# A list planner for attention plus FFN on one core: products picked by how they divide the array, a bias table built from low words, a flag computed inside the stream

## The chip, the cores and the metric

The kernel runs on one core of a Trainium2 chip. The metric is the device time of one launch in microseconds (us). The engines are PE (TensorE), DVE (VectorE), ACT (ScalarE), POOL (GpSimd) and SP (SyncE, which issues most DMAs). Every engine runs its own instructions in the order in which the program emitted them, and waits where an instruction's input or buffer is not ready.

## The reference

Attention with a causal window of 96 keys and 8 global keys, then a mixture of experts, then a second feed-forward network (FFN). B=2, H=8, S=768, head size 64; 4 experts 512 to 1024 to 512; last FFN 512 to 2048 to 512; everything in 32-bit floats.

```python
scores = scale * np.matmul(q, k.transpose(0, 1, 3, 2))
dist = np.where(is_global & ~is_local, float(n_local), np.abs(rel))
scores = scores - slopes[:, None, None] * dist
scores = np.where(is_global | is_local, scores, -1e9)
a = np.exp(scores - scores.max(-1, keepdims=True))
x = np.matmul(a / (a.sum(-1, keepdims=True) + 1e-09), v)      # to (1536, 512)
p = domain_probs / (domain_probs.sum(-1, keepdims=True) + 1e-09)
for e in range(4):
    out += p[:, e:e + 1] * (np.maximum(x @ w1[e], 0.0) @ w2[e])
h = out @ w_in
result = (h * np.clip(h + 3.0, 0.0, 6.0) / 6.0) @ w_out
```

## The kernel before

**Attention** is cut into 24 pairs of heads and query rows, in the order i = 0 to 23: batch b, then head pair hp, then chunk c of 256 rows (c 0 to 2 for the first batch, 3 to 5 for the second). A tile such as `at_4_3` is that of chunk 4, head pair 3. Each pair goes through these pieces: a load of q and k (`qkraw`, L323) and of v (L330) on SP; scores on PE (L351, operands of 64 rows in the two row halves of the array, `att_q<-qkraw 64*128`); bias, mask and minimum on DVE (L366); exponentials on ACT (L381); sums of the weights plus 1e-9, and reciprocals, on DVE (L392, L393); division on POOL (L401); transposes of the weights on PE (L420, the whole array, 128*128, called "turn"); copies of them out of PSUM (L437, ACT for one head's block and DVE for the other, L442 on ACT where the block is short); the product with v on PE (L457, 64 columns, the two column halves); a copy of its result to `xf` on ACT. A pair with c = 0 or 3 is "mixed": its first block sees 128 keys instead of 232, so its products are fewer.

**FFN.** A 32-bit product is made of three products of `fp32r` halves: high with high, low with high, high with low (L909, L913, L916 for the first layer, which runs 7 products for 8 by sums of operands, `wsum`, `xsum`; L1088, L1091, L1092 for the second). Weights and activations are split by a cast on ACT (L250: `w1h`, `w2h`, `xoh`, `hh`) and a subtraction on DVE (L255: `w1l`, `w2l`, `xol`, `hl`). The first layer of the first batch needs the 12 pairs of that batch; the remaining pairs run between its products. 4 experts and then the last FFN follow, in steps of a first and a second layer; from 97.04 us PE runs nothing but these products.

**The order** is made by `Plan`. Every piece of work has an engine, an assumed cost, predecessors and a rank. `emit` simulates the engines with these assumed costs (plus `LATENCY` between engines, `LOAD` behind a load), takes on each engine the ready piece of lowest rank, and emits it. Where the simulated PE would be idle by over 0.4 us, `keep_warm` emits dummy products (L263, `idle`) at that place in PE's stream. The result is one fixed order for each engine.

**The start and the end.** Sizes (n_global, n_local) come as 64-bit integers, two words each (`lo`, `hi`). DVE makes floats `nv` of both words, then the bias table `base` (L184 to L189, with `qkraw<-in_fast`, a table of distances). A flag says if the sizes fit the fast body; behind the body every engine loads it (L1199) and branches to a slow body if it is 0.

Of the kernel before, what the change touches and what calls it, by code (L numbers as in the profile page):

```python
# [21 lines left out]
P = 128  # L22
# [26 lines left out]
T_SCORES, T_TURN, T_VALUES = (0.95, 1.2), (0.8, 1.05), (0.75, 0.97)  # L49
# [9 lines left out]
class Plan:  # L59
# [8 lines left out]
    LATENCY = 0.25  # L68

    def __init__(self, idle=None):  # L70
        self.pieces = []
        self.ported = set()
        self.idle = idle

    def add(self, engine, cost, emit, after=(), rank=0.0, port=False):

        self.pieces.append((engine, cost, emit, after, rank))
        if port or engine == "pool":
            self.ported.add(len(self.pieces) - 1)
        return len(self.pieces) - 1  # L80
# [9 lines left out]
    def emit(self):  # L90
# [3 lines left out]
        port = 0.0  # L94
        for i, (engine, _, _, after, _) in enumerate(self.pieces):
# [50 lines left out]
def moe_attention_kernel(ctx, tc, qk, vw, sizes, dpt, w1, w2, w_in, w_out, ident_d, fast_d, slow_d, out):  # L146
# [29 lines left out]
    ng, nl, nl4 = nv[:, 0:1], nv[:, 1:2], nv[:, 6:7]  # L176
    flag = const.tile([P, 1], I32, name="flag")
    with tc.manual_schedule(engines={mybir.EngineType.DVE}):
        nc.vector.tensor_copy(nf[:], ni[:])
        nc.vector.scalar_tensor_tensor(out=nv[:, 2:4], in0=lo, scalar=0.0, in1=hi, op0=ALU.is_lt, op1=ALU.add)  # L180
        nc.vector.scalar_tensor_tensor(
            out=nv[:, 0:2], in0=nv[:, 2:4], scalar=4294967296.0, in1=lo, op0=ALU.mult, op1=ALU.add
        )
        nc.vector.tensor_scalar(out=window, in0=rel, scalar1=nl, scalar2=NONE, op0=ALU.is_ge, op1=ALU.mult)  # L184
        nc.vector.tensor_scalar(out=nl4, in0=nl, scalar1=-4.0, scalar2=None, op0=ALU.mult)
        nc.vector.scalar_tensor_tensor(out=window, in0=rel, scalar=-4.0, in1=window, op0=ALU.mult, op1=ALU.add)
        nc.vector.tensor_scalar(out=gidx, in0=gidx, scalar1=ng, scalar2=NONE, op0=ALU.is_ge, op1=ALU.mult)
        nc.vector.scalar_tensor_tensor(out=first, in0=gidx, scalar=nl4, in1=window[:, FAR:], op0=ALU.add, op1=ALU.max)
        nc.vector.scalar_tensor_tensor(  # L189
            out=global_keys, in0=gidx[:, :NG], scalar=nl4, in1=global_keys, op0=ALU.add, op1=ALU.max  # L190
        )
# [22 lines left out]
    def t_mm(n, count):  # L214
        return count * (0.0145 + n / 2400.0)

# [4 lines left out]
    def pools(bx, fast):  # L221
# [70 lines left out]
        def plan_bias(tabs, normalised):  # L292

            made = plan.add("dve", 1.9, lambda: None, (), -2.0)
            for h in range(H):
                for kind in range(2):
                    if h == 0:
                        started[h, kind] = made
                        continue

                    def scaled(h=h, kind=kind):
# [7 lines left out]
                        "pool", 0.46 if kind else 0.3, scaled, [made, normalised[3 * (h // 2) - 3] if h > 1 else None], (h // 2 * CPB - 2) * CH + 0.1 * h + 0.5 * kind  # L309
                    )  # L310

        def plan_pair(i, c, hp, tabs, place_users, normalised, biased, outs, x_bank):
# [43 lines left out]
            s_in = plan.add("pe", T_SCORES[kinds[0]], scores, [loaded] + waits, rank)  # L356
            readers.append(s_in)
            weighed = []
            for qb in range(CH):

                def bias(qb=qb, kind=kinds[qb], used=used[qb]):
# [3 lines left out]
                    for j in range(2):  # L365
                        nc.vector.tensor_tensor_reduce(  # L366
                            out=m["t"][:, qb, j, used], in0=m["s", j][:, qb * WIN : (qb + 1) * WIN][:, used],
                            in1=(base if hp == j == 0 else tabs[:, 2 * hp + j - 1])[:, kind * P : P + kind * WIN],
                            scale=-0.125, scalar=HUGE, op0=ALU.add, op1=ALU.min, accum_out=m["mn"][:, qb, j : j + 1],
                        )  # L370

                after = [s_in, started[2 * hp, kinds[qb]], started[2 * hp + 1, kinds[qb]]]
                e = plan.add("dve", 0.72 if kinds[qb] else 0.5, bias, after + wait_t, rank)
                for su in s_users:
                    su.append(e)
                biased[i].append(e)
# [9 lines left out]
                for j in range(2):  # L386
                    weighed.append(
                        plan.add("act", 0.48 if kinds[qb] else 0.39, lambda j=j, f=exponentials: f(j), [e], rank)
                    )

            def sums():
                nc.vector.tensor_scalar(out=m["sm"][:], in0=m["sm"][:], scalar1=1e-9, scalar2=None, op0=ALU.add)  # L392
                nc.vector.reciprocal(m["sm"][:], m["sm"][:])  # L393

            r = plan.add("dve", 0.4, sums, weighed, rank)
            normal = []
            for qb in range(CH):
                for j in range(2):
# [7 lines left out]
                    normal.append(plan.add("pool", 0.46 if kinds[qb] else 0.32, normalise, [r], rank))  # L406
# [7 lines left out]
            def turn(qb):  # L414
# [10 lines left out]
                plan.add("pe", 0.57 if kinds[qb] else 0.3, lambda qb=qb: turn(qb), normal[2*qb:2*qb+2] + wait_a[qb:qb+1], rank)  # L425
# [36 lines left out]
            v = plan.add("pe", T_VALUES[kinds[0]], values, [e for e, _ in copied] + [v_in, biased[i + 2] if b else outs[i - 2]], rank)  # L462
# [130 lines left out]
        def plan_ffn(attention):  # L593
# [513 lines left out]
            def plan_p(b, g):  # L1107
# [7 lines left out]
                gates[b, g] = (t, plan.add("load", 1.0, load, wait + [gate], 20.0 if b == g == 0 else -1.0), p_users)  # L1115

            def finish(b, last, ends):
# [3 lines left out]
                for d in range(KC):  # L1121
# [3 lines left out]
                    for n, part, after, cols, toks in lot:  # L1125
# [12 lines left out]
                        done.append(e)  # L1138
                        if last:
# [10 lines left out]

            results = {}
# [121 lines left out]
```

## Time and profile before

| what | value |
|---|---|
| time, median of 3 runs (lowest to highest) | 848.01 us (847.74 to 849.63) |
| time of the profiled execution | 847.26 us |
| its span in the trace | 845.2 us |
| PE busy | 833.7 us, 99% of the span |
| DVE, ACT, POOL busy | 78%, 48%, 8% |
| first attention product, first FFN product, first product of the second layer, last product | 4.99, 53.48, 97.04, 838.9 us |

The span is the part of the execution that the trace covers; 2.06 us of the profiled execution lie outside it. Busy shares are means over the whole span: attention, where all engines work together, is the first tenth of it only.

### The profile page before, as it was taken

How to read it: one execution, taken by the hardware profiler on the slowest of the kernel's cores; microseconds unless marked ns; L12 is line 12 of the kernel's file. 1: busy time of each engine (PE TensorE's matmuls, PEld its weight loads, DVE VectorE, ACT ScalarE, POOL GpSimd, SP SyncE). 2: the span in 40 equal slices, each digit the busy share in tenths (PEclk: the TensorE clock that was granted, in tenths of full speed). 3: DMA queues.
4: the chain of work that ended last, by engine and by line, in shares of the span. 5: the costliest groups of instructions: out<-in, count | busy, mean ns of one | idle time of the engine just before them, and what ended most of it. 6: DMA issues, size and time to landing. Idle time of an engine off the chain costs nothing.

```text
span 845.2 us, 13646 instructions
## 1 busy us (share of the span) xinstructions
PE 833.7 (99%) x5090; PEld 763.2 (90%) x5090; DVE 655.2 (78%) x1366; ACT 402.0 (48%) x850; POOL 68.1 (8%) x131
## 2 busy tenths in 40 slices
PE   8999999999999999999999999999999999999997
PEld 6777999999999999999999999999999999999996
DVE  6999989988998977987777688689898766545442
ACT  6998643543433433543333333335666455545441
POOL 5888200000000000000000000000000000000000
PEclk9999999999999999999999999999999999999999
DMA  7873454465565565645656664744452555534302
GB/s 264 314 221 94 175 202 153 138 211 181 166 209 194 165 222 180 204 150 179 216 172 199 208 208 158 234 165 140 174 163 103 172 186 185 190 125 139 136 1 79
DMA packets 56985, 147.34 MB, mean 174 GB/s; under 512 B 6480, under 2 KB 7760, under 8 KB 56912
## 3 DMA queue, kind: packets, MB, share of 16 engines
q1 hardware_dynamic: 56480, 145.69, 52.2%
q8 instruction: 42, 0.69, 0.3%
q10 hardware_dynamic: 432, 0.71, 0.3%
q14 instruction: 31, 0.25, 0.1%
HBM read 109.66 MB, written 36.72 MB: 173 GB/s over the span
## 4 chain that ended last, share of the span: by engine, by line
PE 92%; DMA 3%; DVE 2%; POOL 1%; ACT 1%; issue 0%; SPq 0%; POOLq 0%; DVEq 0%; ACTq 0%
PE o L1091 16%; PE o L1092 15%; PE o L1088 15%; PE x_x L909 8%; PE x_x L913 8%; PE x_x L916 8%; PE w_w L913 6%; PE w_w L916 6%; PE w_w L909 6%; PE att_q L420 2%; PE att_q L351 1%; PE att_q L457 1%; DMA qkraw<-in_qk 1%; DMA w<-qkraw 1%; POOL t L401 1%; PE att_x L457 1%
## 5 line engine op out<-in xcount | busy, mean ns | idle before, releaser
L1091 PE MATMUL o<-hh,w2l 128*128 128x512 f32 (+1 forms) x768 | 259.4, 338 | 0.0
L1092 PE MATMUL o<-hl,w2h 128*128 128x512 f32 (+1 forms) x768 | 259.0, 337 | 0.0
L1088 PE MATMUL o<-hh,w2h 128*128 128x512 f32 (+1 forms) x768 | 257.8, 336 | 0.0
L933 ACT COPY snap<-x_x 128x384 f32<-128x384 f32 x144 | 68.9, 478 | 195.9 <-PE x_x L916 195.7
L946 DVE TENSOR_TENSOR c_c<-w_w,snap 128x384 f32<-128x384 f32 x144 | 80.0, 556 | 104.4 <-ACT w2h L250 58.5
L1092 PEld LDWEIGHTS o<-hl,w2h 128*128 128x128 f32 x768 | 144.4, 188 | 16.0
L1088 PEld LDWEIGHTS o<-hh,w2h 128*128 128x128 f32 x768 | 144.4, 188 | 13.4
L1091 PEld LDWEIGHTS o<-hh,w2l 128*128 128x128 f32 x768 | 144.5, 188 | 12.7
L909 PE MATMUL x_x<-xoh,w1h 128*128 128x384 f32 x384 | 129.7, 338 | 0.1
L916 PE MATMUL x_x<-xoh,w1l 128*128 128x384 f32 x384 | 129.0, 336 | 0.0
L913 PE MATMUL x_x<-xol,w1h 128*128 128x384 f32 x384 | 128.9, 336 | 0.0
L913 PE MATMUL w_w<-xol,w1h 128*128 128x384 f32 x288 | 97.1, 337 | 0.0
L909 PE MATMUL w_w<-xoh,w1h 128*128 128x384 f32 x288 | 97.0, 337 | 0.0
L916 PE MATMUL w_w<-xoh,w1l 128*128 128x384 f32 x288 | 96.8, 336 | 0.0
L250 ACT CAST w2h<-wr 128x1024 fp32r<-128x1024 f32 x48 | 50.4, 1050 | 61.2 <-PE o L1092 59.1
L909 PEld LDWEIGHTS x_x<-xoh,w1h 128*128 128x128 f32 x384 | 72.3, 188 | 3.2 <-issue 0.6
L913 PEld LDWEIGHTS x_x<-xol,w1h 128*128 128x128 f32 x384 | 72.3, 188 | 2.0
L1015 ACT CAST hh<-c_c 128x384 fp32r<-128x384 f32 x96 | 49.4, 514 | 48.3 <-DVE c_c L984 47.8
L916 PEld LDWEIGHTS x_x<-xoh,w1l 128*128 128x128 f32 x384 | 72.0, 188 | 0.0
L250 ACT CAST w1h<-wr 128x512 fp32r<-128x512 f32 x96 | 46.9, 510 | 49.5 <-PE w_w L913 45.7
L255 DVE TENSOR_TENSOR w2l<-wr,w2h 128x1024 fp32r<-128x1024 f32 x48 | 58.5, 1219 | 2.3 <-ACT w2h L250 2.3
L984 DVE SCALAR_TENSOR_TENSOR c_c<-c_c,p 128x384 f32<-128x384 f32 x96 | 53.8, 561 | 3.2
(90 smaller groups left out, 1132.7 us busy)
## 6 DMA issues: line engine op xcount, KB each, us to landing
wr<-in_w SPq DMA_DIRECT2D x64, 512.0 KB, 3.9
wr<-w SPq DMA_DIRECT2D x32, 512.0 KB, 3.5
kept<-w1h SPq DMA_DIRECT2D x24, 512.0 KB, 3.0
kept<-w1l SPq DMA_DIRECT2D x24, 512.0 KB, 4.8
w1h<-kept SPq DMA_DIRECT2D x24, 512.0 KB, 3.7
w1l<-kept SPq DMA_DIRECT2D x24, 512.0 KB, 4.9
qkraw<-in_w_in SPq DMA_DIRECT2D x16, 512.0 KB, 4.3
w<-qkraw SPq DMA_DIRECT2D x32, 256.0 KB, 4.2
```

What stands on the lines that cost most here:

```text
L250: nc.scalar.copy(out_ap, src)
L255: nc.vector.tensor_tensor(out_ap, src, hi_ap.bitcast(F32), op=ALU.subtract)
L909: nc.tensor.matmul(ps_, wh[:, a, cols], xh[:, o, kc, :], start=start and kc == 0, stop=False, skip_group_check=True,)
L913: nc.tensor.matmul(ps_, wh[:, a, cols], xl[:, o, kc, :], start=False, stop=False, skip_group_check=True)
L916: nc.tensor.matmul(ps_, wl[:, a, cols], xh[:, o, kc, :], start=False, stop=last, skip_group_check=True)
L933: nc.scalar.copy(m["n", n][:], m["x"][:, :HT])
L946: nc.vector.tensor_tensor(m[name][:], m["w"][:, :HT], m["n", n][:], op=ALU.add)
L984: nc.vector.scalar_tensor_tensor(out=room_for(), in0=src(), scalar=0.0, in1=p["p"][:, cols], op0=ALU.max, op1=ALU.mult)
L1015: nc.scalar.copy(at(0), room_for())
L1088: nc.tensor.matmul(o, wh, hh, start=first and own and f == 0, stop=False, skip_group_check=True)
L1091: nc.tensor.matmul(o, wl, hh, start=False, stop=False, skip_group_check=True)
L1092: nc.tensor.matmul(o, wh, hl, start=False, stop=end, skip_group_check=True)
```

## The change

Six edits, all in what the planner is told or in when a piece is emitted; the arithmetic of the fast body stays the same.

1. **Modes.** Scores get mode "rows", values "columns", all other products none. PE now picks among its first 12 ready pieces the lowest of rank plus 3.0 where the mode differs from that of the last piece; a change of mode is charged 0.1.
2. **Assumed costs.** `LATENCY` 0.25 to 0.12; scores, values and transposes cheaper; bias pieces one head at a time.
3. **Low words.** The first pass uses the sizes' low words as they are; -4 times n_local is made on ACT; the table's global keys are a piece of their own behind the table; the assumed time of the table goes from 1.9 to 0.9.
4. **First pair.** Its sums are made block by block (two pieces).
5. **Flag.** The exact sizes and the flag are computed in the stream by DVE (`ask`, rank 100); the loads of the flag stand behind the first output copy instead of behind the body.
6. **Loads of the probabilities** (`p`) get ranks 34 and 100 for the first two of the first batch, before 20 and -1.

```diff
-T_SCORES, T_TURN, T_VALUES = (0.95, 1.2), (0.8, 1.05), (0.75, 0.97)
+T_SCORES, T_TURN, T_VALUES = (0.87, 1.15), (0.22, 0.45), (0.65, 0.86)
+SWITCH, SWITCH_RANK = 0.1, 3.0
-    LATENCY = 0.25
+    LATENCY = 0.12
+                if engine == "pe" and now[engine]:
+                    place = min(
+                        range(min(len(now[engine]), 12)),
+                        key=lambda k: now[engine][k][0] + SWITCH_RANK * (self.modes.get(now[engine][k][1]) != mode),
+                    )
+                    if best is None or free[engine] < best[0]:
+                        best = (free[engine], engine, place)
+                    continue
+            if engine == "pe" and self.modes.get(i) != mode:
+                mode = self.modes.get(i)
+                cost += SWITCH
...
+        nc.scalar.mul(nl4, nl_low, -4.0)
+        nc.vector.tensor_scalar(out=window, in0=rel, scalar1=nl_low, scalar2=NONE, op0=ALU.is_ge, op1=ALU.mult)
...
-            made = plan.add("dve", 1.9, lambda: None, (), -2.0)
+            made = plan.add("dve", 0.9, lambda: None, (), -2.0)
+            whole = plan.add("dve", 0.22, with_global, [made], 0.0)
...
-            s_in = plan.add("pe", T_SCORES[kinds[0]], scores, [loaded] + waits, rank)
+            s_in = plan.add("pe", T_SCORES[kinds[0]], scores, [loaded] + waits, rank, mode="rows")
-                e = plan.add("dve", 0.72 if kinds[qb] else 0.5, bias, after + wait_t, rank)
+                for j in range(2):
+                    after = [s_in, started[2 * hp + j, kinds[qb]]]
+                    e = plan.add(
+                        "dve", 0.32 if kinds[qb] else 0.21, lambda j=j, f=bias: f(j), after + wait_t, rank
+                    )
-            r = plan.add("dve", 0.4, sums, weighed, rank)
+            parts = [slice(qb, qb + 1) for qb in range(CH)] if i == 0 else [slice(0, CH)]
+            summed = [
+                plan.add("dve", 0.36, lambda part=part: sums(part), weighed[2 * part.start : 2 * part.stop], rank)
+                for part in parts
+            ]
-                plan.add("pe", 0.57 if kinds[qb] else 0.3, lambda qb=qb: turn(qb), normal[2*qb:2*qb+2] + wait_a[qb:qb+1], rank)
+                plan.add("pe", T_TURN[kinds[qb]], lambda qb=qb: turn(qb), normal[2*qb:2*qb+2] + wait_a[qb:qb+1], rank)
-            v = plan.add("pe", T_VALUES[kinds[0]], values, [e for e, _ in copied] + [v_in, biased[i + 2] if b else outs[i - 2]], rank)
+            v = plan.add("pe", T_VALUES[kinds[0]], values, [e for e, _ in copied] + [v_in, biased[i + 2] if b else outs[i - 2]], rank, mode="columns")
...
-                gates[b, g] = (t, plan.add("load", 1.0, load, wait + [gate], 20.0 if b == g == 0 else -1.0), p_users)
+                gates[b, g] = (t, plan.add("load", 1.0, load, wait + [gate], 34.0 if b == g == 0 else 100.0 if b == 0 and g == 1 else -1.0), p_users)
...
+                        if last and b == B - 1 and d == part == 0:
+                            plan.add(
+                                "act", 0.6, lambda: is_fast.append(nc.values_load(flag[0:1, 0:1], min_val=0, max_val=1)),
+                                [e], -9.0,
+                            )
...
+                plan.add("dve", 1.2, ask, x_ready[1], 100.0)
...
-    is_fast = nc.values_load(flag[0:1, 0:1], min_val=0, max_val=1)
-    with tc.If(is_fast == 0):
+    with tc.If(is_fast[0] == 0):
```

What this does to the orders is seen at three places.

PE, behind the first pair's scores. In the kernel before, `att_q2` and `att_q3` are the scores of pair 1, then `att_q0` and `att_q1` those of pair 2, and the transposes of pair 0 (`t_0_0`) come last:

```order
L351 MATMUL att_q2_250<-qkraw_62 128x232
L351 MATMUL att_q3_251<-qkraw_62 128x232
L263 LDWEIGHTS idle_85
L263 MATMUL w_ps_139<-idle_85 128x192
L263 LDWEIGHTS idle_85
L263 MATMUL w_ps_139<-idle_85 128x192
L351 MATMUL att_q0_210<-qkraw_62 128x232
L351 MATMUL att_q1_211<-qkraw_62 128x232
L351 MATMUL att_q0_210<-qkraw_62 128x232
L351 MATMUL att_q1_211<-qkraw_62 128x232
L420 MATMUL att_q4_282<-qkraw_62,t_0_0_221 128x128 x2
L420 MATMUL att_q5_292<-qkraw_62,t_0_0_221 128x128 x4
```

In the changed kernel the transposes of pair 0's first block stand ahead of pair 1's scores:

```order
L277 LDWEIGHTS idle_82
L277 MATMUL w_ps_136<-idle_82 128x192
L450 MATMUL att_q4_256<-qkraw_62,t_0_0_216 128x128 x2
L372 MATMUL att_q2_260<-qkraw_62 128x232
L372 MATMUL att_q3_261<-qkraw_62 128x232
L372 MATMUL att_q2_260<-qkraw_62 128x232
L372 MATMUL att_q3_261<-qkraw_62 128x232
L450 MATMUL att_q5_272<-qkraw_62,t_0_0_216 128x128 x4
L372 MATMUL att_q0_207<-qkraw_62 128x232
L372 MATMUL att_q1_208<-qkraw_62 128x232
L372 MATMUL att_q0_207<-qkraw_62 128x232
L372 MATMUL att_q1_208<-qkraw_62 128x232
```

So the scores of pairs 1 and 2 moved from ahead of the first transposes to behind them; the dummies between those scores are gone.

SP's queue in the middle of attention. The `qkraw` loads here are those of pairs 9, 10, 11 and 12; before:

```order
L323 DMA qkraw_62<-in_qk 128x624
L589 DMA p_dram_1_140<-gate_142 128x4x12
L1113 DMA p_0_1_459<-p_dram_1_140 128x768
L330 DMA v_0_2_473<-in_vw 128x512
L323 DMA qkraw_62<-in_qk 128x624
L1113 DMA p_0_0_502<-p_dram_1_140 128x768
L330 DMA v_1_2_515<-in_vw 128x512
L323 DMA qkraw_62<-in_qk 128x624
L775 DMA wr2_0_536<-in_w2 128x2x512
L330 DMA v_2_2_570<-in_vw 128x512
L775 DMA wr1_1_582<-in_w1 128x2x512
L323 DMA qkraw_62<-in_qk 128x624
```

And in the changed kernel, where the first row is the loads of pairs 8 and 9:

```order
L344 DMA qkraw_62<-in_qk 128x624 x2
L351 DMA v_2_1_424<-in_vw 128x512
L805 DMA wr1_0_430<-in_w1 128x2x512
L619 DMA p_dram_1_137<-gate_139 128x4x12
L344 DMA qkraw_62<-in_qk 128x624
L351 DMA v_0_2_484<-in_vw 128x512
L351 DMA v_1_2_500<-in_vw 128x512
L1143 DMA p_0_0_511<-p_dram_1_137 128x768
L344 DMA qkraw_62<-in_qk 128x624
L351 DMA v_2_2_545<-in_vw 128x512
L805 DMA wr2_0_556<-in_w2 128x2x512
L344 DMA qkraw_62<-in_qk 128x624
```

The load of `p_0_1` and that of the weights `wr1_1` no longer stand ahead of pair 12's load.

DVE near the end of attention, around the copies of the last transposes (`at_4_3_1` is that of pair 22, `at_5_3_1` that of pair 23); before:

```order
L984 SCALAR_TENSOR_TENSOR t_0_1_0_1407<-x_0_x_965,p_0_0_502 128x384
L255 TENSOR_TENSOR w1l_1_741<-wsum_1_1327,w1h_1_740 128x1024
L946 TENSOR_TENSOR c_0_c12_1437<-w_0_w_1164,snap_0_2_1225 128x384
L984 SCALAR_TENSOR_TENSOR c_0_c12_1437<-c_0_c12_1437,p_0_0_502 128x384
L255 TENSOR_TENSOR hl_0_1072<-c_0_c22_1386,hh_0_1071 128x384
L255 TENSOR_TENSOR hl_0_1072<-t_0_1_0_1407,hh_0_1071 128x384
L437 COPY at_4_3_1_1468<-att_q5_292 128x512
L946 TENSOR_TENSOR c_1_c11_1470<-w_1_w_1450,snap_1_1_1448 128x384
L255 TENSOR_TENSOR hl_0_1072<-c_0_c12_1437,hh_0_1071 128x384
L984 SCALAR_TENSOR_TENSOR c_1_c11_1470<-c_1_c11_1470,p_0_0_502 128x384
L255 TENSOR_TENSOR w1l_2_1435<-wr1_2_1382,w1h_2_1434 128x512
L437 COPY at_5_3_1_1500<-att_q5_292 128x512
```

And in the changed kernel:

```order
L1014 SCALAR_TENSOR_TENSOR t_0_1_0_1384<-x_0_x_998,p_0_0_511 128x384
L467 COPY at_4_3_1_1394<-att_q5_272 128x512
L417 TENSOR_SCALAR sm_5_3_1350<-sm_5_3_1350 128x4
L418 RECIPROCAL sm_5_3_1350<-sm_5_3_1350 128x4
L269 TENSOR_TENSOR hl_0_1142<-c_0_c22_1348,hh_0_1141 128x384
L976 TENSOR_TENSOR c_0_c12_1418<-w_0_w_1130,snap_0_2_1229 128x384
L1014 SCALAR_TENSOR_TENSOR c_0_c12_1418<-c_0_c12_1418,p_0_0_511 128x384
L269 TENSOR_TENSOR hl_0_1142<-t_0_1_0_1384,hh_0_1141 128x384
L269 TENSOR_TENSOR w1l_1_1325<-wr1_1_710,w1h_1_1324 128x512
L269 TENSOR_TENSOR hl_0_1142<-c_0_c12_1418,hh_0_1141 128x384
L269 TENSOR_TENSOR w1l_1_1325<-wr1_1_710,w1h_1_1324 128x256
L269 TENSOR_TENSOR w1l_1_1325<-wsum_1_1367,w1h_1_1324 128x1024
```

The three splits into `w1l_1`, weights of the second expert's step, all stand behind the copy of pair 22; before, the first two (512 and 256) stand some 140 instructions further up, the third just ahead of that copy.

## Rows read from the trace of the kernel before

**Rows 1.** The page: TensorE's granted clock in 40 slices, 9 is full.

```profile
PEclk9999999999999999999999999999999999999999
```

**Rows 2.** Busy time by stage: us, PE, PEld, DVE, ACT, POOL (x), PEclk, DMA share, GB/s.

```profile
4.99:25.38 20.39, 19.06 (x176) 13.69 (x176) 17.68 (x92) 16.15 (x64) 13.93 (x34) 1.00 0.78 261
25.38:53.48 28.10, 27.39 (x279) 20.68 (x278) 25.78 (x107) 27.25 (x96) 21.61 (x43) 1.00 0.98 341
53.48:97.04 43.56, 41.95 (x375) 34.53 (x374) 40.66 (x122) 36.00 (x112) 32.15 (x51) 1.00 0.42 125
97.04:838.90 741.86, 741.72 (x4243) 691.21 (x4242) 570.20 (x1043) 321.07 (x580) 0.00 (x0) 1.00 0.51 170
```

**Rows 3.** Timeline of PE, two stretches of attention: start, us, engine, line, xcount.

```profile
15.34 1.05 PE L351 MATMUL att_q<-qkraw 64*128 64x232 f32 x8
16.32 1.10 PE L457 MATMUL att_x<-at,v 104*64 104x128 f32 x16
17.35 1.09 PE L420 MATMUL att_q<-qkraw,t 128*128 128x128 f32 x8
18.37 0.89 PE L351 MATMUL att_q<-qkraw 64*128 64x128 f32 x8
...
92.14 0.66 PE L420 MATMUL att_q<-qkraw,t 128*128 128x128 f32 x4
92.55 0.42 PE L909 MATMUL w_w<-xoh,w1h 128*128 128x384 f32 x1
```

**Rows 4.** Timeline of the start, all engines, with idle time before and releaser.

```profile
1.05 3.56 PE L199 MATMUL w_ps<-idle 128*128 128x192 bf16 x22 [1.05 <-POOL idle L195]
...
5.84 1.58 PE L263 MATMUL w_ps<-idle 128*128 128x192 bf16 x17
...
7.28 0.40 ACT L381 ACTIVATE t<-t,mn 128x128 f32<-128x128 f32 x1 [4.60 <-DVE mn L366]
...
7.34 1.05 PE L351 MATMUL att_q<-qkraw 64*128 64x232 f32 x8
...
9.13 0.17 DVE L392 TENSOR_SCALAR sm<-sm 128x4 f32<-128x4 f32 x1 [0.99 <-ACT t L381]
...
9.69 1.59 POOL L401 TENSOR_SCALAR t<-t,sm 128x128 f32<-128x128 f32 x4 [2.16 <-DVE sm L393]
...
10.12 1.66 PE L420 MATMUL att_q<-qkraw,t 128*128 128x128 f32 x6 [0.46 <-POOL t L401]
```

**Rows 5.** Timeline of PE around 20 us, where the gate's pieces run on DVE.

```profile
20.83 0.66 PE L457 MATMUL att_x<-at,v 104*64 104x128 f32 x8 [0.52 <-DVE at L437]
```

**Rows 6.** Timeline of PE around the scores of pair 12.

```profile
36.15 0.60 PE L420 MATMUL att_q<-qkraw,t 128*128 128x128 f32 x4
37.45 0.89 PE L351 MATMUL att_q<-qkraw 64*128 64x128 f32 x8 [0.70 <-DMA qkraw<-in_qk]
...
42.23 0.88 PE L457 MATMUL att_x<-at,v 128*64 128x128 f32 x12
```

**Rows 7.** Casts of weights on ACT by line, then dummies in PE's timeline.

```profile
L250 ACT CAST w2h<-wr x2: 1034/1046/1058, 36.0 to 45.2; 128x1024 fp32r<-128x1024 f32 x2
...
49.89 0.58 PE L263 MATMUL w_ps<-idle 128*128 128x192 bf16 x5
```

**Rows 8.** Behind the first FFN product: PE's and DVE's timelines, and low halves on DVE by line.

```profile
62.30 0.63 PE L420 MATMUL att_q<-qkraw,t 128*128 128x128 f32 x4 [1.22 <-DVE at L437]
...
94.83 1.10 PE L457 MATMUL att_q<-at,v 104*64 104x128 f32 x16
...
92.83 0.69 DVE L437 COPY at<-att_q 128x512 f32<-128x512 f32 x1
...
L255 DVE TENSOR_TENSOR w2l<-wr,w2h x2: 1224/1232/1240, 37.0 to 46.4; 128x1024 fp32r<-128x1024 f32 x2
```

**Rows 9.** Loads of the flag behind the body: ns, and when.

```profile
L1199 PEldq TENSOR_LOAD <-flag x1: 758/758/758, 837.3 to 837.3; - x1
...
L1199 ACTq TENSOR_LOAD <-flag x1: 476/476/476, 840.7 to 840.7; - x1
```

More of the change, by code (lines that the diff above doesn't have):

```diff
@@ L72, in __init__, with add @@
         self.ported = set()
+        self.modes = {}
         self.idle = idle
-    def add(self, engine, cost, emit, after=(), rank=0.0, port=False):
+    def add(self, engine, cost, emit, after=(), rank=0.0, port=False, mode=None):
         self.pieces.append((engine, cost, emit, after, rank))
+        if mode:
+            self.modes[len(self.pieces) - 1] = mode
         if port or engine == "pool":
@@ L94, in emit @@
         port = 0.0
+        mode = None
         for i, (engine, _, _, after, _) in enumerate(self.pieces):
@@ L387, in plan_pair, with sums @@
                     weighed.append(
-                        plan.add("act", 0.48 if kinds[qb] else 0.39, lambda j=j, f=exponentials: f(j), [e], rank)
+                        plan.add("act", 0.48 if kinds[qb] else 0.39, lambda j=j, f=exponentials: f(j), [shifted[j]], rank)
                     )
-            def sums():
-                nc.vector.tensor_scalar(out=m["sm"][:], in0=m["sm"][:], scalar1=1e-9, scalar2=None, op0=ALU.add)
-                nc.vector.reciprocal(m["sm"][:], m["sm"][:])
-            r = plan.add("dve", 0.4, sums, weighed, rank)
+            def sums(part):
+                sm = m["sm"][:, part].rearrange("p a b -> p (a b)")
+                nc.vector.tensor_scalar(out=sm, in0=sm, scalar1=1e-9, scalar2=None, op0=ALU.add)
+                nc.vector.reciprocal(sm, sm)
+            parts = [slice(qb, qb + 1) for qb in range(CH)] if i == 0 else [slice(0, CH)]
[3 more added lines that the diff above has]
+            ]
             normal = []
@@ L1149, in finish, with ask @@
                 results[b] = done
+            if fast:
+                def ask():
+                    nc.vector.scalar_tensor_tensor(
+                        out=nv[:, 2:4], in0=lo, scalar=0.0, in1=hi, op0=ALU.is_lt, op1=ALU.add
+                    )
+                    nc.vector.scalar_tensor_tensor(
+                        out=nv[:, 0:2], in0=nv[:, 2:4], scalar=4294967296.0, in1=lo, op0=ALU.mult, op1=ALU.add
+                    )
+                    nc.vector.tensor_scalar(out=nv[:, 4:5], in0=nl, scalar1=1.0, scalar2=None, op0=ALU.is_ge)
+                    nc.vector.scalar_tensor_tensor(
+                        out=nv[:, 5:6], in0=nl, scalar=float(NPREV + 1), in1=nv[:, 4:5], op0=ALU.is_le, op1=ALU.mult
+                    )
+                    nc.vector.scalar_tensor_tensor(
+                        out=nv[:, 5:6], in0=ng, scalar=-2147483648.0, in1=nv[:, 5:6], op0=ALU.is_ge, op1=ALU.mult
+                    )
+                    nc.vector.scalar_tensor_tensor(
+                        out=flag[:], in0=ng, scalar=float(NG), in1=nv[:, 5:6], op0=ALU.is_le, op1=ALU.mult
+                    )
+                plan.add("dve", 1.2, ask, x_ready[1], 100.0)
             results = {}
```

51 lines of the change are left out of this document (20 added, 31 removed).

## The prediction

> **What bounds the kernel now.** I began with the stages [rows 2]. From 97.04 us to the last product PE is busy 741.72 of 741.86 us, so nothing that the change does there can shorten the time, unless it takes away products, and it takes away none. What can move are the 92 us before: three stretches in which PE is idle 1.33, 0.71 and 1.61 us, and in which some groups are stretched besides. PE is still the engine that paces them, but ACT is at 97% in the second stretch (27.25 of 28.10) and DVE at 93% in the third (40.66 of 43.56). Next I read PE's timeline for the price of a group, start to next start [rows 3]: scores 0.98 us, values 1.03, eight transposes 1.02, scores of a mixed pair about 0.82 and values of one 0.81 (estimates by their count of columns). Four transposes ahead of a whole-array product take 0.41; twice that is 0.82, so leaving the whole array after eight costs about 0.20. I then followed the start [rows 4], the copy that PE waits for at 20.8 [rows 5], the load at 37 [rows 6], the casts [rows 7], the waits behind the first FFN product [rows 8] and the end [rows 9].
>
> **The start: later, +1.0.** Before, the four exponentials of pair 0 run from 7.28 in the order 128, 128, 232, 232, and their sums start at 9.13; POOL divides from 9.69 (0.40 each), PE transposes from 10.12 [rows 4]. The new order is 128, 232, 128, 232 and sums per block, so the first block's sums wait for the third exponential: 7.28 + 0.40 + 0.48 + 0.40 = 8.6 with its read-out. 0.56 from sums to POOL gives 9.2, two divisions 10.0, the two transposes follow the divisions. The low words bring nothing here: the table waits for its distances, which land only at 5.40, and without the flag's interleaved instructions the first bias is at most 0.2 sooner. What moves is the other side: pair 1's scores stood ahead of those transposes at 7.34, now they stand behind them, at 10.2. PE idles from the end of the dummies (7.4) to about 9.7. In the prices of rows 3: 10.2 + scores 0.98 + four transposes 0.59 + scores 0.98 gives values of pair 0 at 12.8 (before 12.5), then mixed scores, two more score groups and two transpose groups, and values of pair 1 at 17.7 (before 16.32) [rows 3]. That is +1.4. Before, PE waits 0.52 at 20.83 for a copy that stands behind the gate's pieces on DVE [rows 5]; a later PE finds it done, which returns 0.5. I take +1.0. Bounds: 0 (the waits of this stretch, 1.33 idle plus stretched groups, absorb all) and +2.9 (10.2 less 7.34, nothing regained).
>
> **25 to 53 us: −1.5.** The load of pair 12's q and k has one load of probabilities (393 KB) and one of weights (512 KB) fewer ahead of it: 905 KB at this stretch's 341 GB/s [rows 2] is 2.65 us, more than the 0.70 that PE waits for it [rows 6]. From 36.15 to the values at 42.23 PE spends 6.08 us on two score groups, one values group and fourteen transposes, which cost 0.98 + 0.82 + 1.03 + 14 x 0.128 + 0.2 for their pieces = 4.8 by rows 3; 1.3 goes. The order also moves the two `w2h` casts (2.1 us of ACT) behind the first FFN product, with their low halves on DVE (2.5 us) [rows 7, 8]. ACT sets PE's waits where dummies stand in the stream, the five at 49.89 the largest (0.5); I give 0.9 for these. New waits: a copy behind a 1024-wide subtraction on DVE and values of pair 14 behind theirs, 0.35 each by the timeline, 0.7. Sum −1.5. Bounds −2.2 (no new waits) and 0.
>
> **53 to 97 us: −0.2.** The moved casts and subtractions fall here. Waits that go: 1.22 at 62.30 and the rest of the 1.61 idle [rows 2, 8], with the stretched groups some 2.4. Waits that come, from the order: transposes of pair 18 behind their sums (0.6), the copy behind `w2l` (1.23, of which 0.35 is not covered), the products of the second step behind `w1l_1`, which now stands behind the copy of pair 22 and four other pieces (0.95 of 0.5 + 1.3 not covered), the last copy (0.35). 2.25 against 2.4. Six first-layer products (78 before, 72 now) move behind the first second-layer product; at 0.175 (741.86/4243) that shifts 1.05 us from one side of that point to the other and changes no time. Bounds −2.1 (all old waits gone, no new) and +2.4 (all come on top).
>
> **Grouping: inside these terms.** I counted PE's changes of mode up to the second layer in the two orders: 82 and 78, of which leaving the whole array 35 and 33. Two times 0.20 is 0.4; where a group merges, its waits merge too, so −0.1 is in the sums above and 0.4 is the bound of this edit. The Trainium skill, TensorEngine Tiling (Array Packing), section "Key Properties", says that a change of tiling mode drains TensorE, without a figure. If each of the four changes cost the 0.20 of the row, the sum would be 0.7 lower; the trace shows the cost at leaving the whole array only, so that is a part of rival C.
>
> **The end: −0.5.** Before, ACT loads the flag at 840.7, behind its output DMA, 0.48 us [rows 9], and its branch is the last thing of the span. Now the load is behind the first output copy, beside products; PE's own sequencer reached it at 837.3, 1.6 us ahead of its last product, so a load inside the stream stops no product. Bounds −0.5 and 0. The six flag instructions in DVE's stream (0.15 each, 1 us) come behind x of the second batch, at about 97, where DVE is 77% busy.
>
> **Sum.** +1.0 − 1.5 − 0.2 − 0.5 = −1.2. The profiled execution took 847.26, so 846.1; the median of the runs stands 0.75 above it, and the median should go from 848.01 to 846.8.
>
> **Rivals.**
> *B, DVE becomes the bound after the first FFN product (slower).* That product comes 2.8 us later (56.2), and 2.5 us of low halves plus the rest come with it into a stretch that is 93% busy. If DVE reaches some 97%, its pieces are late one after the other: the last copy, at 92.83, comes at 96.1, and the last values, 94.83 [rows 8], at 96.2, +1.3; with the six products that are then behind instead of ahead, 1.05, and the end's −0.5, +1.9: 849.9. For it: the DVE share. Against it: PE waited for DVE once only.
> *C, the late start is caught up.* PE idles anyway in the first stretch, and groups merge. Then +1.0 is 0 to 0.3, and the later terms reach two thirds of their bounds: 843.4 to 845.5. For it: more pieces per block, so less idling behind sums; against it: PE shows 19.06 of 20.39 busy, little room.
> *D, the clock falls at the start.* The granted clock is full in all slices [rows 1], that is the upper of 1.2 and 2.4 GHz, and before the longest idle of PE is 1.22. Yet the first 22 dummies took 0.162 each, the 17 later 0.093 [rows 4]. The new order lets PE idle 2.3 us at 7.4. If products again run at the early pace for 3.56 us, 1.5 is lost: 848.3. The Trainium skill, TensorE: Matmul & The Clock Gate, section "Why this matters for your kernels", warns that idle gaps of PE lower the clock; no row before shows it.
> *E, no change that adds up*: the planner's new costs move waits and remove none, 848.0.
>
> **How the numbers follow.** Forecast 0.45 (its own range 845.3 to 848.3), C 0.22, B 0.17, D 0.08, E 0.08. A measurement of this kernel tells 0.2%, 1.7 us, from nothing: faster is under 846.3, slower over 849.7. Faster: all of C and two fifths of the forecast, 0.40. Slower: most of B and the forecast's upper edge, 0.17. The rest 0.43. The range 843.4 to 849.6 goes from C's low end to just short of B.
>
> **What would show it.** Start right: pair 1's scores near 10.2 with 2.3 of PE idle before, values of pair 1 near 17.7. Second stretch right: no DMA wait before pair 12's scores, first FFN product near 56. Third: first product of the second layer near 95.3 (97.04 − 1.05 − 0.7). End: the last product near 838, ACT's last instruction the output DMA. Wrong: scores of pair 1 still near 7 or PE clock under full at 8 to 12 (D); last values past 96 with DVE at 97% (B); the second layer before 94 (C).

## The result: 1.2% slower, most of it in one place at 700 us

The changed kernel took 859.09 us (median of 4 runs, 857.25 to 860.48) against 848.1 for the kernel before on the same chip: ratio 1.0123, 95% interval 1.011 to 1.0137. The forecast was 846.8, range 843.4 to 849.6. The profiled execution took 859.32, its span is 857.1 against 845.2: 11.9 us more.

The page of the changed kernel shows where to look. Its line of PE in 40 slices (21.4 us each) has two eights in slices 33 and 34, where the kernel before has nines:

```profile
PE   8999999999999999999999999999999988999997
PEclk9999999999999999999999999999999999999999
```

The windows, cut at the same events as [rows 2] (first scores, the same set of groups as at 25.38 before, first FFN product, first product of the second layer) and further at the gap; the columns are those of rows 2:

```profile
5.01:26.65 21.64, 18.21 (x169) 13.32 (x169) 16.13 (x86) 14.48 (x56) 13.27 (x33) 1.00 0.81 250
26.65:57.76 31.11, 30.56 (x317) 23.29 (x316) 26.27 (x117) 29.73 (x113) 24.60 (x51) 1.00 0.90 288
57.76:98.69 40.93, 38.63 (x334) 31.01 (x334) 38.31 (x114) 35.37 (x102) 27.55 (x44) 1.00 0.44 135
98.69:699.95 601.26, 601.15 (x3439) 559.78 (x3438) 491.45 (x907) 249.72 (x448) 0.00 (x0) 1.00 0.53 176
699.95:716.46 16.51, 11.50 (x43) 10.00 (x42) 9.71 (x20) 6.89 (x14) 0.00 (x0) 0.79 0.51 189
716.46:850.00 133.54, 133.54 (x762) 124.00 (x763) 69.51 (x125) 64.36 (x119) 0.00 (x0) 1.00 0.38 129
```

From 98.69 to 699.95 and from 716.46 on PE is as full as before. Between them 42 products took 16.51 us, which at 0.174 each are 7.3: 9.2 us lost. PE's timeline there, from the last product before the wait:

```profile
699.78 0.28 PE L1122 MATMUL o<-hl,w2h 128*128 128x256 f32 x1
702.02 0.44 PE L939 MATMUL x_x<-xoh,w1h 128*128 128x384 f32 x1 [1.96 <-ACT w1h L264]
702.30 0.35 PE L943 MATMUL x_x<-xol,w1h 128*128 128x384 f32 x1
702.75 0.69 PE L946 MATMUL x_x<-xoh,w1l 128*128 128x384 f32 x1
703.23 0.52 PE L939 MATMUL x_x<-xoh,w1h 128*128 128x384 f32 x1
703.55 0.52 PE L943 MATMUL x_x<-xol,w1h 128*128 128x384 f32 x1
...
706.19 0.34 PE L943 MATMUL x_x<-xol,w1h 128*128 128x384 f32 x1
708.64 0.45 PE L946 MATMUL x_x<-xoh,w1l 128*128 128x384 f32 x1 [2.11 <-DVE w1l L269]
```

PE waits for the weights of one step, first for their high half (`w1h`, 1.96), then for low halves (`w1l`, 2.11); two shorter waits of 0.57 and 0.28 follow. Behind each of the two long waits products start 0.32 us apart instead of 0.175; some 20 of them in the gap, 2.9 us. The granted clock, third number from the right in the windows, is at the lower of its two levels there, 1.2 of 2.4 GHz:

```profile
699.95:702.75 2.80, 0.74 (x4) 0.30 (x3) 1.58 (x5) 0.93 (x2) 0.00 (x0) 0.95 0.68 265
702.75:705.90 3.15, 3.15 (x10) 3.05 (x10) 2.07 (x5) 1.42 (x2) 0.00 (x0) 0.50 0.03 5
705.90:709.30 3.40, 1.29 (x8) 0.97 (x7) 3.01 (x5) 1.34 (x3) 0.00 (x0) 1.00 0.39 154
709.30:712.70 3.40, 3.40 (x12) 3.40 (x11) 1.33 (x3) 1.10 (x3) 0.00 (x0) 0.50 0.59 231
```

What is late is read in the chain of waits, followed back from there:

```profile
691.07 0.70 DVE qkraw L750
691.79 0.44 DVE qkraw L755
692.25 0.70 DVE qkraw L761
692.98 0.70 DVE qkraw L773
693.70 4.05 DMA w<-qkraw
697.80 3.48 DMA wr<-w
701.34 0.30 issue
```

These lines lie in a piece that front and prediction don't mention. `w_in` and `w_out` arrive as 64-bit numbers. 32 **conversions** make 32-bit ones of them: a load, seven DVE instructions (L731 to L773, 4.0 us together), a store to DRAM (`w`), one after the other through one buffer. In the planner they have the last rank, 100000 + n, so they fill what the planner takes for DVE's spare time over the 700 us behind attention. Step 39 (counted from 0; the last of the final FFN's first half) loads its first-layer weights from the 31st. In the kernel before, this conversion's last DVE instruction ended at 670.2, in the changed one at 693.7; then the store, the load (7.5 us by the chain), the split.

That is not lateness of the last few only. DVE's work up to 580 us, in the kernel before and in the changed one:

```profile
97.04:580.00 482.96, 482.96 (x2765) 450.58 (x2765) 403.05 (x736) 187.50 (x340) 0.00 (x0) 1.00 0.57 185
```

```profile
97.04:580.00 482.96, 482.85 (x2768) 450.01 (x2765) 394.43 (x732) 188.92 (x341) 0.00 (x0) 1.00 0.56 184
```

DVE (the third busy time) has done 8.6 us less at the same time, two conversions: the kernel before ended its 28th at 580.3, the changed one its 26th at 582.6.

The rest: first product of the second layer at 98.69 with 72 products of the first layer ahead of it, so 99.74 beside 97.04 (six times 0.175 for the moved ones), +2.7. The end: 6.31 us from the last product's start (850.75) to the end of the span, 6.57 before (838.61), −0.26. Sum 2.7 + 9.4 − 0.26 = 11.9; 9.4 is all behind 98.69, the 9.2 of the gap included. This is the difference of two traced executions, and that of the kernel before was a short one: its span was 845.2, its median span in the later sets of runs 846.6 to 847.0. By the ratio the change costs 10.4, so what the rest of the stream adds to the 9.4 is nearer 1 than 2.4.

### The profile page after: what moved, and what is told of

It is laid out like the page before. It is cut to its first block, busy times and chain, and to the rows that moved or that the text cites. A ratio compares the mean times of both kernels' runs of the same rounds, so it can differ in the third digit from the quotient of the medians.

```text
span 857.1 us, 13657 instructions
## 1 busy us (share of the span) xinstructions
PE 838.3 (98%) x5085; PEld 765.4 (89%) x5085; DVE 652.0 (76%) x1368; ACT 402.8 (47%) x851; POOL 65.9 (8%) x131
## 4 chain that ended last, share of the span: by engine, by line
PE 90%; DVE 5%; DMA 3%; ACT 1%; issue 1%; SPq 0%; POOL 0%; ACTq 0%; DVEq 0%
PE o L1122 15%; PE o L1121 15%; PE o L1118 15%; PE x_x L946 8%; PE x_x L939 8%; PE x_x L943 8%; PE w_w L939 6%; PE w_w L943 6%; PE w_w L946 6%; PE att_q L450 2%; PE att_q L372 1%; PE att_x L487 1%; DVE t L386 1%; DMA wr<-in_w 1%; ACT t L405 1%
```

## The experiments

The median for the kernel before was 848.1 to 849.5 from one set of runs to the next, so each time stands as a ratio to the kernel before in the same set, with its 95% interval. Of each time 1.5 to 2.5 us lie outside the span: 2.1 to 2.4 for the kernel before, 1.8 for the same kernel with nothing but dearer conversions. So some 0.6 us of a difference in time need not be one of the stream. "Behind 97" is the time from the first product of the second layer to the last product of the profiled execution, with 0.175 for each product moved across that point, less the same of the kernel before (741.6).

**Undo LATENCY, or do it alone.** The changed kernel with the old value, and the kernel before with the new one:

```diff
-    LATENCY = 0.12
+    LATENCY = 0.25
```

> The changed kernel with LATENCY 0.25, all else as changed. The order of the conversions falls back to that of the kernel before from the twelfth on. Theory A: no wait at 700 us; 848 to 850.5, by what the attention order costs. Rival B (DVE cannot carry it, or the attention part costs by itself): 855 or more.

Measured: ratio 1.0016 (1.0004 to 1.0027), no wait behind 97 (−0.4). The 31st conversion ended at 674.1. Theory A.

> The kernel before with LATENCY 0.12 alone. Its conversions stand one place behind those of the kernel before from the eighteenth on, and the last one stands one first-layer result later. Theory A: a part of the wait at 700 us comes, 849 to 854, and the first FFN product stays within 1.5 us of 53.5. Rival C (only the new costs of the attention products make the conversions late, the latency does nothing): 848.0, no wait near 700.

Measured: ratio 1.0053 (1.0034 to 1.0073), 7.2 us behind 97: this number alone makes a wait at 705.1 in the kernel before (3.2 us, for a combination on DVE, at the start of step 40) with twelve slow products behind it. The 31st conversion ended at 682.7. Rival C falls. That this wait, too, comes from the conversions is shown by the run under "A miss" below.

**Convert the last ones earlier.** First all of a conversion's pieces for n from 27 on, then only those on DVE:

```diff
-                rank = 1e5 + n
+                rank = 1e5 + n if n < 27 else 150.0 + n
```

> The changed kernel with one edit: the last five of the 32 conversions of w_in and w_out (64-bit to 32-bit, on DVE) get rank 150+n instead of 100000+n; the orders are the same up to there. Theory A (the planner put these conversions so late that the last step of the final FFN's first half waits for its weights at 700 us, and TensorE's clock falls behind that wait): the gap at 700 us and the slow products after it are gone, 859.1 less 9.2 = about 849.9 (849.3 to 850.6). Rival B (DVE or SP as a whole cannot carry this work in time, the wait only shows there): the wait moves to another step, 855 or more.

Measured: 859.63, ratio 1.0125 (1.009 to 1.016). The 31st conversion ended at 662.5, but PE waited from 669.9 for 3.4 us, with slow products behind it: in step 37, two steps earlier, so the wait moved, as rival B had it. What PE waited for is a cast of operand sums (`wsum`), which stand on DVE behind the instructions of the 32nd conversion:

```profile
670.07 0.69 DVE L761 SCALAR_TENSOR_TENSOR qkraw<-qkraw 128x512 f32<-128x512 uint32 x1
671.14 0.68 DVE L773 TENSOR_TENSOR qkraw<-qkraw 128x512 f32<-128x512 f32 x1
671.75 0.42 DVE L862 TENSOR_TENSOR wsum<-wr,wsum 128x256 f32<-128x256 f32 x1
672.20 1.05 ACT L264 CAST w1h<-wsum 128x1024 fp32r<-128x1024 f32 x1 [1.95 <-DVE wsum L862]
```

SP's queue was held as well: a store waited 9.3 us for DVE, with two weight loads behind it, but the chain of this wait does not lead there. The edit had also moved the stores forward, since their rank is the conversion's less 10000. So the next try left loads and stores alone:

```diff
-                    last = plan.add("dve", costs[j], step, [last] + (waits if j == 0 else []), rank, port=True)
+                    last = plan.add("dve", costs[j], step, [last] + (waits if j == 0 else []), 229.5 + n // 4, port=True)
...
```

The seventh instruction gets the same rank.

> The changed kernel; only the DVE pieces of the conversions get a rank that follows the step that needs them (229.5 plus the step's number within the last FFN), their loads and stores keep their ranks, so no store stands in SP's queue ahead of loads that do not depend on it. In the orders the 29th to 32nd conversion end 4, 4, 5 and 3 first-layer results earlier than in the changed kernel. Theory A (lateness of these conversions is the cause; the first try put the stores ahead of weight loads and the conversions ahead of the next step's sums): no wait of TensorE over 1 us behind 97 us, no slow products, ratio to before 1.002 to 1.005. Rival B (DVE and SP as a whole cannot carry the work by then): a wait of 3 us or more again between 640 and 720, ratio 1.009 or more.

Measured: ratio 1.009 (1.0073 to 1.0107); the waits stand at 670 to 683 (2.1 the longest), 5.9 us behind 97. The ratio is rival B's, though no wait reaches its 3 us, and the clock stayed full. Theory A as I had put it falls: with two conversions missing at 580, neither of two orders behind that point avoids the wait. DVE is busy for 97 to 98 us of the 110 from 580 to 690 in these runs, 94.7 in the kernel before.

**Convert early.** The new theory (A2): the two conversions have to be done while DVE has room, before 580. The words "DVE is full from 600 to 680" below are too strong: it is busy there for 68.30 of 80 us in the kernel before. No run separates DVE's share from the one buffer, through which a conversion's load and store take some 4 us each besides.

```diff
-                    last = plan.add("dve", costs[j], step, [last] + (waits if j == 0 else []), rank, port=True)
+                    last = plan.add("dve", costs[j], step, [last] + (waits if j == 0 else []), (200.0 + 6.5 + n if n < 24 else rank), port=True)
...
```

Again the seventh instruction gets the same rank.

> The changed kernel, LATENCY 0.12 and all; only the DVE pieces of the first 24 conversions get rank 206.5+n, so that they stand about a place earlier from the thirteenth on and the last five stand exactly where the kernel before has them. Theory A2 (DVE time that stands unused between 100 and 580 us, two conversions of 4.1 us, cannot be had back later, since DVE is full from 600 to 680): DVE is busy some 8 us longer between 100 and 580 us, no wait of TensorE over 1 us behind 97 us, ratio 1.002 to 1.0045 (what the attention part costs). Rival B2 (LATENCY itself makes the last FFN's own pieces stand in a worse order): a wait near 700 us again, ratio 1.006 or more.

Measured: ratio 1.0025 (1.0013 to 1.0036), with LATENCY still 0.12. DVE's work up to 580 is back, and PE has no gap in the stretch where it had one:

```profile
97.04:580.00 482.96, 482.93 (x2768) 450.05 (x2765) 403.90 (x745) 189.03 (x341) 0.00 (x0) 1.00 0.57 187
580.00:690.00 110.00, 110.00 (x632) 102.67 (x631) 93.72 (x174) 63.87 (x114) 0.00 (x0) 1.00 0.44 151
690.00:720.00 30.00, 30.00 (x172) 27.95 (x171) 19.03 (x36) 15.60 (x31) 0.00 (x0) 1.00 0.56 200
```

0.1 us behind 97 instead of 9.4. The ratio falls from 1.0123 to 1.0025: some 8 of the 10.4 us (1.23% of 848) are the conversions.

**Late conversions in the kernel before.** The reverse: the attention order and LATENCY as before, conversions dearer for the planner (six of the seven instructions).

```diff
-                costs = (0.43, 0.69, 0.42, 0.75, 0.43, 0.7)
+                costs = tuple(1.1 * c for c in (0.43, 0.69, 0.42, 0.75, 0.43, 0.7))
```

> The kernel before; the planner takes the conversions' DVE pieces for 10 per cent longer than before, nothing else. TensorE's order is the same up to product 3451 of the FFN, and the last conversions stand where the changed kernel has them (28th to 32nd: one place late, 31st at the same place). Theory A2: a wait of TensorE near 700 us, slow products behind it, ratio 1.005 to 1.011. Rival G (the attention order or LATENCY is needed for the wait): 1.000, no wait behind 97 us.

Measured: ratio 1.0025 (1.0014 to 1.0036), 1.8 us behind 97, no slow products. Right in sign, a third of the size: the order was that of the changed kernel, but in time the 31st conversion ended at 687.1, 6.6 us sooner than there. So 20 per cent:

> The kernel before; the planner takes the conversions' DVE pieces for 20 per cent longer, so that the last five stand later than in the changed kernel (the 29th to 31st all at one place, three first-layer results behind where the kernel before has the first of them). Theory A2 (the wait grows with the lateness alone): a wait of TensorE between 670 and 720 us larger than the changed kernel's, slow products behind it, ratio 1.012 to 1.035. Rival H (the 10 per cent run's 1.8 us is all that lateness can do, the changed kernel's 9.4 needs LATENCY besides): ratio 1.002 to 1.005.

Measured: ratio 1.0294 (1.0277 to 1.031); the 31st conversion ended at 709.3, and PE waited 17.9 us for the same weights. Windows, then the waits of PE:

```profile
97.00:580.00 483.00, 483.00 (x2766) 450.65 (x2765) 391.08 (x714) 187.09 (x340) 0.00 (x0) 1.00 0.55 181
580.00:690.00 110.00, 108.55 (x622) 101.05 (x620) 88.09 (x164) 60.68 (x108) 0.00 (x0) 1.00 0.41 139
690.00:720.00 30.00, 11.59 (x56) 9.76 (x57) 15.95 (x31) 1.31 (x4) 0.00 (x0) 0.72 0.36 114
```

```profile
PE x_x L909 <- ACT w1h L250: 17.9, 1, 17.9
```

So lateness of the conversions, with attention's order and LATENCY as before, is enough for a wait longer than the changed kernel's; behind it the clock fell here too (717.4 to 726.9). Their end and the loss, in runs in which the conversions have no rank of their own:

| kernel | DVE busy 97 to 580 | 31st conversion ends | lost behind 97 |
|---|---|---|---|
| changed, old LATENCY | 404.2 | 674.1 | −0.4 |
| before | 403.1 | 670.2 | 0 |
| before, conversions +10% | 399.2 | 687.1 | 1.8 |
| changed, old costs (below) | 397.3 | 685.6 | 2.6 |
| before, new LATENCY | 397.2 | 682.7 | 7.2 |
| changed | 394.4 | 693.7 | 9.4 |
| before, conversions +20% | 391.1 | 709.3 | 26.9 |

The loss grows row by row as DVE's work up to 580 shrinks; in the four runs not in the table, all below, DVE's work is 401.5 to 405.6 and the loss −0.4 to 0.4. The end of the 31st conversion follows it less closely: with the new LATENCY alone the wait is another one, for a combination on DVE.

**Which number loses the two conversions.** Three parts of the change can be taken back, the costs, the pick by mode and LATENCY:

```diff
-T_SCORES, T_TURN, T_VALUES = (0.87, 1.15), (0.22, 0.45), (0.65, 0.86)
-SWITCH, SWITCH_RANK = 0.1, 3.0
+T_SCORES, T_TURN, T_VALUES = (0.95, 1.2), (0.3, 0.57), (0.75, 0.97)
+SWITCH, SWITCH_RANK = 0.0, 0.0
...
-    LATENCY = 0.12
+    LATENCY = 0.25
```

The first run takes back the costs and LATENCY (so the pick is left), the second the pick and LATENCY (the costs are left), the third the costs alone.

> The changed kernel with LATENCY 0.25 and the old costs; the pick of TensorE's pieces by mode stays. The conversions stand exactly as in the kernel before. Theory A: no wait behind 97 us; the pick by itself moves under 1.5 us either way, ratio 0.998 to 1.002. Rival E (the pick holds back transposes on which the FFN waits): ratio 1.003 or more.

Measured: ratio 1.0083 (1.0066 to 1.01), and none of it behind 97 (−0.4): 9.9 us in attention. Rival E in sign, but by another way than I had written. With these costs the planner puts a cast of `w2h` into ACT's queue far ahead of its data, and ACT's copies and exponentials stand behind it; the chain of waits, 30 to 40 us:

```profile
27.56 6.98 DMA wr<-in_w
34.54 0.02 issue
34.56 1.04 ACT w2h L264
35.60 0.27 ACT at L472
35.87 0.48 ACT t L405 x2
36.35 0.27 ACT xf L497
36.62 0.04 issue
36.67 1.54 PE att_x L487 x12
```

PE is idle for 2.91 us in front of that last row. But the wait is not all of the 9.9. The granted clock was at its lower level twice, behind an idle stretch of 1.40 at 8.4 and behind this one:

```profile
12.03:15.44 3.41, 3.41 (x26) 2.45 (x26) 1.72 (x11) 3.03 (x13) 1.38 (x4) 0.50 0.10 19
35.92:42.75 6.83, 6.08 (x32) 4.38 (x34) 2.94 (x12) 5.72 (x20) 1.76 (x4) 0.50 0.62 227
```

PE's 9.5 us of work there at half the clock make some 4.7 of the loss (an estimate: half of them).

> The changed kernel with LATENCY 0.25 and without the pick by mode; the three new costs stay. The conversions stand one place later until the twelfth, from then as before. Theory A: no wait behind 97 us, the lost place is made good by the planner; ratio 0.999 to 1.003. Rival F (a place lost early is never made good on the chip): a wait near 700 us, ratio 1.004 or more.

Measured: ratio 1.002 (1.0008 to 1.0031), no wait behind 97. The place lost early is made good where LATENCY is old.

> The changed kernel with the three old costs, so LATENCY 0.12 and the pick by mode stay. The conversions stand as in the run of the kernel before with the new latency: one place late from the eighteenth on. Theory A: that run's wait (3.5 us at 705) and slow products come again, ratio 1.004 to 1.007, less than the changed kernel's 1.0125 where the new costs lose a second place. Rival C (the wait hangs on latency alone, the costs add nothing): ratio 1.009 or more.

Measured: ratio 1.0052 (1.0035 to 1.0068), 2.6 us behind 97 and 3.0 in attention. The ratio is in theory A's range, but half by luck: the wait at 708 is 1.2 us, with no slow products, and the 3.0 in attention make up the rest. What the run does show is that LATENCY with the pick loses less than LATENCY, the pick and the costs (2.6 against 9.4): LATENCY loses one place, the new costs a second, which the planner made good with the old LATENCY.

**The start.** The kernel with early conversions, and the table's assumed time back:

```diff
-            made = plan.add("dve", 0.9, lambda: None, (), -2.0)
+            made = plan.add("dve", 1.9, lambda: None, (), -2.0)
```

> The kernel of the run before this one with the bias table's assumed time back at 1.9: pair 1's scores stand ahead of pair 0's transposes again. Theory S (the later start costs 1.3 us to 26 us, and some of it stays): 0.5 to 1.5 us less than the run before this one. Rival T (the time of the start is absorbed by later waits): the same within 0.4 us.

Measured: ratio 0.9995 (0.9984 to 1.0007), 849.08 against 851.24 in the same set of runs: 2.2 us less, above the range expected. Pair 1's scores stand ahead of the transposes again (9.64 in its timeline against 10.71), and the orders further on differ too.

**Old planner, new rest.** All three numbers and the pick as before:

> The changed kernel with LATENCY, the three costs and the pick on TensorE as before; left of the change are the low words, the bias pieces by head, the sums by block, the flag in the stream and the ranks of the p loads. Theory A: conversions stand as before, no wait at 700 us, and pair 1's scores run ahead of pair 0's transposes again; 847.5 to 849. Rival B: a wait at 700 us stays, 853 or more.

Measured: ratio 0.9984 (0.9971 to 0.9997), no wait behind 97.

> The kernel of the fourth experiment once more, against the kernel before in five rounds: LATENCY, costs and pick as before; low words, bias by head, sums by block, flag in the stream, ranks of the p loads as changed. If its 0.9984 was real: 0.997 to 0.9993, part of it the end of the stream, 0.26 us shorter. If it was the spread of the runs: 0.9993 to 1.001.

Measured: ratio 0.9984 (0.9976 to 0.9993) in twelve runs, 1.6 us. By the median spans it is 1.1 (845.5 against 846.6); the other 0.5 lies outside the span, where the kernel with dearer conversions is shorter by 0.35 too. The two traced executions, of 845.6 and 846.6, are not below the 845.2 of the kernel before. A gain of about 0.1% is likely; where it comes from is open.

**A miss.** The new LATENCY in the kernel before, with the early conversions:

> The kernel before with LATENCY 0.12 and the same rank for its first 24 conversions. Theory A2: the wait of the run with the new latency alone (ratio 1.0053) is gone; what is left is its attention order, 0.5 us shorter than before by its trace: ratio 0.998 to 1.0005. Rival B2: 1.003 or more.

Measured: ratio 1.0027 (1.001 to 1.0045), 1.0 us behind 97 instead of 7.2, the 31st conversion at 673.9. The wait is gone, as A2 says, but the ratio lies between the two ranges: its second layer begins 2.4 us later by the same measure that gave −0.5 to the run with LATENCY alone, 2.9 between two kernels of one attention order. The traces show where: 1.4 are there by the first FFN product (55.88 against 54.48), from a slower start (the first eight score products 1.57 us against 1.14, the 17 dummies 2.65 against 1.58). The other 1.5 come behind an idle stretch of 1.2 at 82.3, with the clock at its lower level from 84.2 to 87.6. The run with conversions 10 per cent dearer has the same slow start, with PE's order as before, and there the second layer begins 1.4 later than in the kernel before. So single traces of one order differ by that much, and no difference in attention below it can be given to an edit from one trace.

## Why the prediction was wrong

**The step that failed** is in the first paragraph: "nothing that the change does there can shorten the time", after which only "the 92 us before" were costed. The sentence is true and looks one way. PE is full from 97 on only as long as every step's weights are ready, and what makes them ready is planned with the same LATENCY. The change moves 700 us of DVE's order, and I read that order near the end of attention only. The windows had the hint: DVE busy for 570 of 742 us behind 97, which I used once and for another thing. No rival had this mechanism; B, the rival on the other side, had DVE as the bound at 53 to 97 and 849.9. In place of the zero behind 97 stand 9.4 us: two conversions late at 580, weights late at 700, and the clock's fall behind the waits. Putting the conversions back early takes the loss there to 0.1, the ratio from 1.0123 to 1.0025.

**The attention terms.** The sum up to the second layer was −0.7, measured +2.7, of which up to 1.4 can be a matter of the two executions that were traced.
- Start +1.0: the set was done at 26.65 against 25.38, +1.3; the mechanism was right. The transposes wait 1.93 where I had 2.3, pair 1's scores run at 10.40 (10.2). The timeline of PE, which answers to rows 4 and 5:

```profile
9.79 0.68 PE L450 MATMUL att_q<-qkraw,t 128*128 128x128 f32 x2 [1.93 <-POOL t L431]
10.40 1.05 PE L372 MATMUL att_q<-qkraw 64*128 64x232 f32 x8
...
18.14 1.10 PE L487 MATMUL att_x<-at,v 104*64 104x128 f32 x16
...
23.08 0.63 PE L450 MATMUL att_q<-qkraw,t 128*128 128x128 f32 x4 [1.47 <-DVE sm L417]
```

  Values of pair 1 came at 18.14 (17.7). The wait behind the gate's pieces did not go, as I had it, but became 1.47 at 23.08: the gate's pieces began at 20.36 instead of 18.06, since their load was issued at 16.23 instead of 14.29.
- 25 to 53, −1.5: in the changed kernel 8 score products, 10 transposes and 16 value products more stand ahead of the first FFN product, 3.3 by the prices of rows 3. 57.76 less 3.3 is 54.5, +1.0 against 53.48, so this stretch gave back 0.3. The part that was looked at in SP's order held: pair 12's scores have no wait any more. What I had not priced: PE's groups wait for copies and dummies at other places (0.39 at 54.83).

```profile
41.23 0.89 PE L372 MATMUL att_q<-qkraw 64*128 64x128 f32 x8
...
54.83 0.66 PE L487 MATMUL att_q<-at,v 104*64 104x128 f32 x8 [0.39 <-DVE at L467]
```

- 53 to 97, −0.2: +1.7 (2.7 less 1.0). The wait for `w1l` that the order showed came (0.74, I had 0.95), three for divisions and `xoh` of 0.3 to 0.4 that I had not seen. The old waits did not all go. (The bounds in the prediction do not follow from its terms, which give −2.4 and +2.25; nothing hangs on it.) Rival B's DVE share was 94% (38.31 of 40.93), not 97%.
- The end −0.5: −0.26. ACT's load is out of the way (844.1), but a gain is not shown: the stretch from the last product to the end took 6.3 to 8.7 us in the five traces with the old end and 5.9 to 8.0 in the eleven with the new.

```profile
L1171 PEldq TENSOR_LOAD <-flag x1: 488/488/488, 841.8 to 841.8; - x1
L1171 ACTq TENSOR_LOAD <-flag x1: 470/470/470, 844.1 to 844.1; - x1
```

**Grouping.** The pick by mode, 0.1 to 0.4 by the rows, did not show as a gain in any run. With old costs and old LATENCY attention took 9.9 us longer than before; the run that differs from it by the pick alone ("old planner, new rest") took 0.5 longer. Between them lie the wait on ACT and the clock's fall at 35.9. The rule of drains (the Trainium skill, TensorEngine Tiling (Array Packing), section "Key Properties") was no guide to the sign: no run isolates its price, and what moved with the pick was larger.

**The clock, rival D.** No fall after the 1.93 us of idle at 7.9 (scores of 1.05 at 10.40, as before), so D did not come there in the changed kernel. It came at 700, twice, at the lower level for 3.4 us each; its 2.9 us are a third of the gap. And four runs show it where I had put it, behind only 1.3 to 1.4 us of idle at 8.4: the changed kernel with the old LATENCY, the one with the pick alone, and both runs of the old planner with the new rest, from whose first trace this is:

```profile
10.73:14.14 3.41, 3.41 (x18) 2.18 (x19) 1.59 (x6) 2.27 (x10) 1.43 (x5) 0.50 0.23 85
```

Half of 3.41 is 1.7 lost (an estimate), close to D's 1.5. The mechanism of D is real here; that it stayed away from the start of the changed kernel's traced execution is luck, as far as these runs tell.

## What to carry to other kernels

A planner's number that is changed for one stage changes the order of every stage it plans: read the new order on every engine to the end, above all the pieces of last rank, and ask of each chain of fillers when its last link is due. "PE is full there" says that nothing can be gained, not that nothing can be lost. Work that fills spare time has to keep ahead of its due time early, while there is room: promoted late, it only moved the wait.

## What was not expected of the hardware

Idle stretches of PE of nearly the same length had different ends. In the changed kernel the next products ran at their usual pace after 1.93 us at 7.9; after 1.96 us at 700, which followed 600 us of full work, ten products started 0.32 us apart, at a granted clock of 0.50. The fall came 2.4 us after the idle began, when PE was at work again, and lasted 3.4 us. In other runs the clock fell behind 1.3 to 1.4 us of idle at 8.4 and behind 1.2 at 82.3, and did not fall behind 2.0 at 7.7. So the length of the idle stretch by itself does not tell; what does, these runs do not show. Among the four runs of the changed kernel, too, the longer one had the lower mean granted clock: 857.25, 858.85, 859.32 and 860.48 us at 0.997, 0.996, 0.995 and 0.994. The waits in the run with late conversions promoted on DVE alone (four, the longest 2.1 us, between 670 and 683) brought no slow products at all.
